# Eight places for weight steps in a gated batch, an early first chunk, and a re-ordered channel MLP

## The chip, the cores and the metric

The kernel runs on one core of one Trainium2 chip. The metric is the time of the device in microseconds (us), smaller is better; the outputs have to match the reference within float32-like accuracy, which the kernel reaches by splitting each float32 operand of a matmul into a high and a low part ("fp32r" in the rows) and multiplying three combinations.

## The reference

Three layers follow each other on 8 batches of 576 positions and 512 channels (8 heads of 64).

```
k_p, q_p = phi(k), phi(q)                       # linear attention, 128 features, exp(+-)
attn = (q_p @ (k_p.T @ v)) / (q_p . sum(k_p))
h = relu(x @ w_in); u, v = h[..., :512], h[..., 512:]
v_s = w_spatial @ layernorm(v) + b_spatial      # mixes positions
x = (u * v_s) @ w_out                           # gated MLP
u = x + (x.T @ U @ V).T                         # rank 32 mix of positions
out = u + relu(u @ w_ch1) @ w_ch2               # channel MLP, 512 -> 2048 -> 512
```

## The kernel before

**Stages.** The program is one straight line of instructions. The attention ends at about 388 us of the span. Then come eight gated batches, b0 to b7, of some 65 us each, and from 925 us the channel MLP.

**A gated batch.** On TensorE (PE): `pu` (x times w_in for u; ACT applies the relu, L907), then `pz` (w_spatial times the normalized v). DVE multiplies `pz` by u in place (L928), and ACT and POOL split the product into the parts of `gs` (L146, L149). Then `px` (gs times w_out) for four tiles of 128 positions and a fifth of 64, which shares a product with its low part (L790; "tail" below). ACT copies each px into x (L960), DVE splits x into xh and xl (L148, L149), and PE goes on with the rank 32 mix: `pr` (L974, L976), `pt` and `py` (L996 to L1000), the sum going to DRAM as `ud`. The values `v` of the next batch (`pv`, L839 to L856) lie between. A scheduler places these stages; within an engine the order is fixed once the kernel is built.

**Weight steps.** The channel MLP's weights have to be expanded from an integer form, split and written to DRAM beside the batches. `channel_jobs` makes lists of jobs per batch: *pieces* of w_ch1 and rows of w_ch2 (each a DMA in, L53; ACT L62 and L80; DVE L67, L71, L75, L87; a DMA out, L359), *pairs* (two such fetches, sums on POOL L457, a split into `w2s` in two parts that share one buffer, each stored as `w2d`, L415) and *lefts* (the same sums and splits for w_ch1, `w1s`, stored to `w1x`, L439). `work()` pops one step; `gate` calls it once per f in its first loop (4 calls) and, in its second loop, once per f but the last (3 calls), with one more step pending per pair of calls.

**Channel MLP.** It is a two-level scheme with 7 products each way. For each of 16 chunks n, `channel` issues the outer products `pc` from the left parts w (a DMA w<-w2d, L1286) and the right parts `hc` (hidden values split, L146, L149). Between them it pulls steps of the generator `inner`, which makes the hidden values of the coming chunk: for each of 4 tiles t, seven products into two PSUM tiles, X (`ph_x`, products 0, 1, 3, 6) and Y (`ph_y` with product 4, then `ph_z` with 2 and 5). X is read after each of its first three products by ACT (copies s1, u2, u3, L1148), DVE adds such a copy to Y (c, L1153), and ACT writes relu(c) or relu(X) into `h` (L1161). The chunk's input u (DMA u<-ud, 1152 KB) is summed on POOL (t, L1089) and split into `us` (ACT L146, DVE L149) by `right_parts`, a generator whose steps are taken at the places (t, i) of a table, `spread` (`begin` for the first chunk). `second_group` loads, sums and splits the next left parts (ca, cs, cd) for half the chunks; `channel` takes its steps at 7 of 14 places (`later`). `rest` adds the products in DRAM terms (r, L1320). In this stage every engine's instructions are pinned to the program's order.

Of the kernel before, what the change touches and what calls it, by code (L numbers as in the profile page):

```python
# [18 lines left out]
P = 128  # L19
# [81 lines left out]
class Mixer:  # L101
# [243 lines left out]
    def channel_jobs(self):  # L345
# [99 lines left out]
        todo = [jobs[4 * m : 4 * m + 4] + [pair(m)] for m in range(GROUP)]  # L445
        todo += [jobs[4 * GROUP :], [left(m) for m in range(GROUP)]]
# [438 lines left out]
    def gate(self, b, jobs):  # L885
# [27 lines left out]
        for f in range(self.KH):  # L913
# [20 lines left out]
            if f < self.KH - 1:  # L934
                self.work()
# [151 lines left out]

    def less(self, out, p, q):
        self.put(self.nc.gpsimd.tensor_tensor(out=out, in0=p, in1=q, op=ALU.subtract))  # L1089
        return out  # L1090
# [36 lines left out]
    def hidden(self, n, m):  # L1127
# [55 lines left out]
        keep(3, c22[0])  # L1183
        keep(2, X)
        yield
# [4 lines left out]
    def inner(self):  # L1190
# [5 lines left out]
        for k in range(total):  # L1196
# [5 lines left out]
            for k, i in (  # L1202
                (0, 1), (1, 0), (0, 2), (1, 1), (0, 3), (1, 2), (0, 4), (1, 3), (1, 4),
                (0, 5), (0, 6), (1, 5), (1, 6), (2, 0),
# [6 lines left out]
                (2, 2), (2, 4), (2, 5), (3, 2), (3, 3), (3, 4), (4, 0), (3, 5), (4, 1), (4, 3),  # L1211
            )
        }
        for k, i in order:
# [13 lines left out]
            if (t, i) == (2, 2) and u is not None:  # L1228
                right, u = self.right_parts(n + 1, u), None
            at, steps = (k, i), begin  # L1230
            if k > GROUP + 1 or k == GROUP + 1 and i < 5:
                at, steps = (t, i), spread
                if t == 0 and (GROUP, i) in spread:
                    at = (GROUP, i)
            for _ in range(steps.get(at, 0)):
                next(right, None)
# [54 lines left out]
    def channel(self, inner):  # L1291
# [5 lines left out]
        for _ in range(7 * GROUP + FIRST - 7 * EARLY):  # L1297
            next(inner, None)
# [3 lines left out]
        def fill(f, into, n):  # L1302
            while len(into) < n:
                d = next(f, None)
                if d is None:
                    break
                into.append(d)
# [31 lines left out]

        fill(weights, ws, 5)  # L1340
        rest(0, 0, 0)
        rest(0, 0, 1)
        for n in range(total):
            for x in OUTER:
# [30 lines left out]
                for t in range(GROUP):  # L1375
# [19 lines left out]
                    if n and at in range(0, 14, 2):  # L1395
                        next(later, None)
# [3 lines left out]
def favor_gmlp_mixer_kernel(ctx: ExitStack, tc: tile.TileContext, **aps):  # L1400
# [11 lines left out]
    todo = [late] + jobs + [[]]  # L1412
    for t in range(NST):
        mx.values(0, t)
    for b in range(B):
        last = b == B - 1
        mx.gate(b, todo[b])
        if last:
            right.close()
            mx.alloc_channel(ctx)  # L1420
            u = mx.load_chunk(0)
            for m in range(GROUP):
                mx.load_left(m)
            right_parts = mx.right_parts(0, u)
            inner = mx.inner()
        else:
            for kk in range(KD):
                mx.load_x(b + 1, kk)()()
# [118 lines left out]
```

## Time and profile before

| | us |
|---|---|
| median of 3 runs (lowest, highest) | 1654.58 (1654.47, 1655.69) |
| the profiled execution | 1655.13 |
| span of its trace, from the first to the last instruction | 1653.3 |
| busy in the span: PE, DVE, ACT, POOL | 1574.3, 1177.9, 879.0, 793.9 |
| mean granted clock of PE | 0.992 |

The table is read from the top: the profiled execution lies 0.55 us above the median, inside the spread of the runs, so its rows stand for them. PE is busy 95% of the span, and no other engine comes near that. A granted clock of 1 is 2.4 GHz, 0.5 is 1.2 GHz.

### The profile page before, as it was taken

The page shows a single profiled execution, that of the slowest core. Times are in us where ns is not written, and L with a number is a line of the kernel's source. Part 1 is how long each engine was busy: PE and PEld are TensorE (multiplying, and loading weights), DVE is VectorE, ACT ScalarE, POOL GpSimd, SP SyncE. Part 2 cuts the span into 40 slices and gives each one's busy share as a digit, 9 for nine tenths or more (in the row PEclk, how much of TensorE's full clock was granted, in tenths as well). Part 3 has the DMA queues.
Part 4 walks back from the last instruction along what each step waited for, and adds up shares of the span by engine and source line. Part 5 has one row for each costly group of instructions (what it writes and reads, how often), then busy time and mean ns, then how long its engine had stood idle before and what let it go on. Part 6 is the DMA issues. An engine that isn't in the chain of part 4 may idle for free.

```text
span 1653.3 us, 30606 instructions
## 1 busy us (share of the span) xinstructions
PE 1574.3 (95%) x11592; PEld 1467.8 (89%) x11592; DVE 1177.9 (71%) x1642; ACT 879.0 (53%) x1668; POOL 793.9 (48%) x610
## 2 busy tenths in 40 slices
PE   7999999998999999898999899999999999999998
PEld 7998889888888787796988899999999999999998
DVE  6888757865576776757455678878877777767765
ACT  5888768773444444434434555555554455445443
POOL 3677766774342442442533346545543444433342
PEclk9999999999999999999999999999999999999999
DMA  4676666642252442523526668998899777777776
GB/s 136 194 205 203 201 186 179 197 141 70 70 162 88 144 147 88 173 89 121 193 84 249 226 222 267 317 325 293 298 330 389 258 223 225 244 251 234 250 240 231
DMA packets 172182, 336.72 MB, mean 204 GB/s; under 512 B 25794, under 2 KB 96610, under 8 KB 168964
## 3 DMA queue, kind: packets, MB, share of 16 engines
q1 hardware_dynamic: 171892, 334.72, 63.0%
q8 instruction: 91, 1.49, 0.4%
q14 instruction: 55, 0.45, 0.1%
q10 hardware_dynamic: 144, 0.07, 0.0%
HBM read 251.58 MB, written 73.55 MB: 197 GB/s over the span
## 4 chain that ended last, share of the span: by engine, by line
PE 53%; DVE 17%; DMA 14%; ACT 8%; issue 4%; POOL 2%; SPq 1%; DVEq 0%; ACTq 0%; POOLq 0%
PE pc L778 12%; PE ph_x L778 7%; PE pn L615 5%; PE pv L778 4%; PE pu L778 4%; PE pkv L587 4%; PE ph_z L778 4%; DVE hc L149 3%; DVE us L149 3%; DMA w<-w2d 2%; DMA w2d<-cd 2%; PE ph_y L778 2%; PE pk L514 2%; PE pt L546 2%; DMA raw_c<-in_w_ch 1%
## 5 line engine op out<-in xcount | busy, mean ns | idle before, releaser
L778 PE MATMUL pc<-hc,w 128*128 128x288 f32 x2688 | 422.4, 296 | 6.7 <-ACT hc L146 2.8
L778 PEld LDWEIGHTS pc<-hc,w 128*128 128x128 f32 x2688 | 379.2, 188 | 8.8 <-ACT hc L146 4.5
L778 PE MATMUL ph_x<-us,cw 128*128 128x288 f32 x1536 | 247.1, 296 | 9.8 <-ACT u L1148 7.0
L568 POOL TENSOR_TENSOR qp<-e,qp 128x576 fp32r<-128x576 f32 x128 | 183.9, 1458 | 121.1 <-ACT e L565 84.6
L778 PEld LDWEIGHTS ph_x<-us,cw 128*128 128x128 f32 x1536 | 217.6, 188 | 14.4 <-ACT u L1148 10.9
L615 PE MATMUL pn<-qp,kv 128*65 128x288 f32 x768 | 208.1, 331 | 10.2 <-DVE nd L624 6.7
L1089 POOL TENSOR_TENSOR t<-h,h 128x576 f32<-128x576 f32 x64 | 94.2, 1473 | 233.0 <-DVE hc L149 203.4
L149 DVE TENSOR_TENSOR hc<-t,hc 128x576 fp32r<-128x576 f32 x128 | 129.8, 1016 | 63.2 <-ACT hc L146 63.1
L1161 ACT ACTIVATE h<-c 128x288 f32<-128x288 f32 x192 | 85.7, 446 | 148.1 <-DVE c L1153 148.0
L587 PE MATMUL pkv<-v,kp 128*128 128x65 f32 x1024 | 153.8, 253 | 0.0
L587 PEld LDWEIGHTS pkv<-v,kp 128*128 128x128 f32 x1024 | 152.6, 192 | 0.0
L778 PE MATMUL ph_z<-us,cw 128*128 128x288 f32 x768 | 126.6, 299 | 8.6 <-DVE c L1153 8.4
L1148 ACT COPY u<-ph_x 128x288 f32<-128x288 f32 x128 | 51.0, 398 | 150.0 <-PE ph_x L778 149.9
L778 PEld LDWEIGHTS ph_z<-us,cw 128*128 128x128 f32 x768 | 107.8, 188 | 13.4 <-DVE c L1153 10.7
L1089 POOL TENSOR_TENSOR t<-h,t 128x576 f32<-128x576 f32 x64 | 113.1, 1768 | 8.3 <-DVE hc L149 5.8
L149 DVE TENSOR_TENSOR hc<-h,hc 128x576 fp32r<-128x576 f32 x96 | 115.6, 1208 | 1.9 <-ACT hc L146 1.9
L1089 POOL TENSOR_TENSOR t<-u 128x576 f32<-128x576 f32 x32 | 49.8, 1558 | 136.0 <-DVE us L149 116.6
L615 PEld LDWEIGHTS pn<-qp,kv 128*65 128x65 f32 x768 | 99.2, 140 | 16.2 <-DVE nd L624 8.1
L778 PE MATMUL pz<-wt,vn 128*128 128x288 f32 x768 | 112.6, 295 | 0.9 <-DVE u L928 0.9
L149 DVE TENSOR_TENSOR us<-t,us 128x576 fp32r<-128x576 f32 x64 | 85.0, 1331 | 36.1 <-ACT us L146 35.3
L778 PE MATMUL pu<-xs,wi 128*128 128x288 f32 x768 | 105.5, 299 | 4.3 <-DVE v L842 4.3
L778 PEld LDWEIGHTS pu<-xs,wi 128*128 128x128 f32 x768 | 104.9, 191 | 5.3 <-DVE v L842 4.5
(169 smaller groups left out, 3193.2 us busy)
## 6 DMA issues: line engine op xcount, KB each, us to landing
w<-w2d SPq DMA_DIRECT2D x224, 512.0 KB, 4.8
u<-ud SPq DMA_DIRECT2D x16, 1152.0 KB, 5.6
raw_c<-in_w_ch SPq DMA_DIRECT2D x32, 512.0 KB, 4.1
cw<-w1x SPq DMA_DIRECT2D x8, 1792.0 KB, 10.8
v<-in_v SPq DMA_DIRECT2D x32, 325.0 KB, 4.1
k<-in_kT SPq DMA_DIRECT2D x32, 320.0 KB, 3.5
q<-in_qT SPq DMA_DIRECT2D x32, 320.0 KB, 3.7
x<-nd SPq DMA_DIRECT2D x64, 144.0 KB, 3.2
```

The costliest lines, as they stand in the source:

```text
L149: return self.put((nc.gpsimd if elo == "pool" else nc.vector).tensor_tensor(out=lo, in0=src, in1=hi, op=ALU.subtract))
L514: self.pin(nc.tensor.matmul(pa[:, j * NF + t, :], x[d, t * P : (t + 1) * P], ws[d, :], start=True, stop=True,))
L546: self.pin(nc.tensor.transpose(pt[:, at, :], s[:, u, :], self.ident))
L568: self.pin(nc.gpsimd.tensor_tensor(out=lo[:, c], in0=e[:, c], in1=hi[:, c], op=ALU.subtract))
L587: self.pin(nc.tensor.matmul(pkv[:, i, j, :], kp[:, j * NF + t, :], vb[:, u * D1 : (u + 1) * D1], start=False, stop=(j == 1 and t == NF - 1),))
L615: self.pin(nc.tensor.matmul(pn, kv[k][:, i, g // 2, :], qp[q][:, i, g * HS : (g + 1) * HS], start=(m == 0), stop=(m == len(terms) - 1),))
L778: self.put(self.nc.tensor.matmul(out, x, y, start=(start and i == 0), stop=(stop and i == len(terms) - 1), skip_group_check=chained,))
L1089: self.put(self.nc.gpsimd.tensor_tensor(out=out, in0=p, in1=q, op=ALU.subtract))
L1148: self.put(nc.scalar.copy(out, src))
L1161: self.put(nc.scalar.activation(self.h[n, t // 2, x][:, t % 2], src, AF.Relu))
```

## The change

Eight edits: (A) `channel_jobs` deals its jobs to the batches in another way: b0 gets the remainder of an earlier job list plus two pieces, b1 to b4 three pieces and a pair each, b5 seven pieces, b6 three pieces and two lefts, b7 (nothing before) two lefts. (B) The second loop of `gate` calls `work()` after the first two f only. (C) `first_chunk` loads the first chunk's u into the buffer of the last batch's xs, and not into a buffer of its own. (D) In `hidden` the relus of X and of c22 are issued one product later, X's first. (E) Two neighbours in `inner`'s early order are exchanged. (F) `right_parts` of the coming chunk is made at (1, 6) and not at (2, 2), and its steps are taken at other places. (G) The first outer form is filled after the 23rd step of the channel's early pulls, not after all of them. (H) `second_group`'s steps come at other places of 14.

```diff
@@ -442,8 +442,9 @@
                 return (lambda: part(w, z, 1)) if k == 0 else None
             return load
 
-        todo = [jobs[4 * m : 4 * m + 4] + [pair(m)] for m in range(GROUP)]
-        todo += [jobs[4 * GROUP :], [left(m) for m in range(GROUP)]]
+        lefts = [left(m) for m in range(GROUP)]
+        todo = [jobs[:2]] + [jobs[3 * m + 2 : 3 * m + 5] + [pair(m)] for m in range(GROUP)]
+        todo += [jobs[14:21], jobs[21:] + lefts[:2], lefts[2:]]
         return todo
 
     def left_sums(self, blocks, z):
@@ -931,7 +932,7 @@
                 lo = self.split(gs[:, 0, f, cs], gs[:, 1, f, cs], u, elo=elo)
                 self.last[2 if elo == "pool" else 1] = lo.ins
 
-            if f < self.KH - 1:
+            if f < self.KH - 2:
                 self.work()
         self.gs, self.gt = gs, self.last_tokens(self.mp, gs, f"gt_{b}")
 
@@ -1083,6 +1084,12 @@
     def load_chunk(self, n):
         u = self.hu.tile([P, self.KD, self.S], F32, tag="u32", name=f"u32_{n}", bufs=1)
         self.nc.sync.dma_start(u, self.ud[n % self.B])
+        return u
+
+    def first_chunk(self):
+
+        u = self.wp.tile([P, 2, self.KD, self.S], F32, tag="xs", name="u32_0", bufs=1)[:, 0]
+        self.nc.sync.dma_start(u, self.ud[0])
         return u
 
     def less(self, out, p, q):
@@ -1180,9 +1187,7 @@
         c22 = []
         yield lambda: c22.append(plus(Y, u3))
         product(X, 6, False, True)
-        keep(3, c22[0])
-        keep(2, X)
-        yield
+        yield lambda: (keep(2, X), keep(3, c22[0]))
         product(Y, 5, False, True)
         c12 = plus(Y, u2)
         yield lambda: keep(1, c12)
@@ -1200,15 +1205,15 @@
         order[a:z] = [
             (EARLY + k, i)
             for k, i in (
-                (0, 1), (1, 0), (0, 2), (1, 1), (0, 3), (1, 2), (0, 4), (1, 3), (1, 4),
-                (0, 5), (0, 6), (1, 5), (1, 6), (2, 0),
+                (0, 1), (1, 0), (0, 2), (1, 1), (0, 3), (1, 2), (0, 4), (1, 3), (0, 5),
+                (1, 4), (0, 6), (1, 5), (1, 6), (2, 0),
             )
         ]
         pairs, late, right, u = {}, None, iter(()), None
         begin = {(2, 3): 1, (2, 5): 1, (2, 6): 1, (3, 6): 2, (4, 0): 2, (4, 2): 1, (4, 3): 1, (4, 4): 1}
         spread = {
             x: 1 for x in (
-                (2, 2), (2, 4), (2, 5), (3, 2), (3, 3), (3, 4), (4, 0), (3, 5), (4, 1), (4, 3),
+                (1, 6), (2, 3), (2, 6), (3, 2), (3, 3), (4, 0), (3, 5), (3, 6), (4, 1), (4, 3),
             )
         }
         for k, i in order:
@@ -1225,13 +1230,13 @@
             late = after
             if (t, i) == (1, 1) and n + 1 < groups * B:
                 u = self.load_chunk(n + 1)
-            if (t, i) == (2, 2) and u is not None:
-                right, u = self.right_parts(n + 1, u), None
             at, steps = (k, i), begin
-            if k > GROUP + 1 or k == GROUP + 1 and i < 5:
+            if k > GROUP:
                 at, steps = (t, i), spread
                 if t == 0 and (GROUP, i) in spread:
                     at = (GROUP, i)
+            if at == ((2, 3) if steps is begin else (1, 6)) and u is not None:
+                right, u = self.right_parts(n + 1, u), None
             for _ in range(steps.get(at, 0)):
                 next(right, None)
             if i == 6 and (n + 1) % B == 0 and g + 1 < groups:
@@ -1294,8 +1299,6 @@
         nc, HS, B, S = self.nc, self.HS, self.B, self.S
         total = self.NM // GROUP * B
         self.pinning = True
-        for _ in range(7 * GROUP + FIRST - 7 * EARLY):
-            next(inner, None)
         forms, weights, later = self.operands(), self.outer_weights(), self.second_group()
         ready, ws, rs = [], [], {}
 
@@ -1337,6 +1340,10 @@
         def banks(name, tag):
             return self.ps["c"].tile([P, 2, 512], F32, tag=tag, name=name, bufs=1)[:, :, :HS]
 
+        for i in range(7 * EARLY, 7 * GROUP + FIRST):
+            next(inner, None)
+            if i == 22:
+                fill(forms, ready, 1)
         fill(weights, ws, 5)
         rest(0, 0, 0)
         rest(0, 0, 1)
@@ -1392,7 +1399,7 @@
                         pulls += (LEAD - FIRST) // 4
                     for _ in range(pulls):
                         next(inner, None)
-                    if n and at in range(0, 14, 2):
+                    if n and at in (1, 3, 5, 6, 9, 11, 12):
                         next(later, None)
 
 
@@ -1409,7 +1416,7 @@
 
     mx.alloc_moe(left, right)
     jobs = mx.channel_jobs()
-    todo = [late] + jobs + [[]]
+    todo = [late + jobs[0]] + jobs[1:]
     for t in range(NST):
         mx.values(0, t)
     for b in range(B):
@@ -1418,7 +1425,7 @@
         if last:
             right.close()
             mx.alloc_channel(ctx)
-            u = mx.load_chunk(0)
+            u = mx.first_chunk()
             for m in range(GROUP):
                 mx.load_left(m)
             right_parts = mx.right_parts(0, u)
```

**ACT, batch b1.** Before: x products of b1 are copied at L960 (px, four tiles); g is the split of gs, gt a copy of its last part, w2 and z2 the two sources of the pair's store.

```order
L146 CAST g_1_5553<-u1_2_5471 128x288
L62 ACTIVATE low_c2_0_1_5684<-raw2_c2_0_1_5638 128x512
L146 CAST g_1_5553<-u1_3_5512 128x288
L80 ACTIVATE low_c2_0_1_5684<-raw2_c2_0_1_5638 128x512
L146 CAST g_1_5553<-u1_3_5512 128x288
L800 COPY gt_1_5733<-g_1_5553 128x4x64
L146 CAST w2s_0_0_5933<-w2_0_5599 128x512
L800 COPY gt_1_5733<-g_1_5553 128x4x64
L146 CAST w2s_0_0_5933<-w2_0_5599 128x256
L146 CAST w2s_0_1_6003<-z2_0_5692 128x1024
L960 COPY x_1_0_5783<-px1_0_5753 128x512
L960 COPY x_1_1_5792<-px1_1_5763 128x512
```

ACT at the same place after the change (lines of after from L442 on are higher by one or more):

```order
L146 CAST g_1_5577<-u1_2_5495 128x288
L62 ACTIVATE low_c2_0_1_5660<-raw2_c2_0_1_5614 128x512
L146 CAST g_1_5577<-u1_2_5495 128x288
L80 ACTIVATE low_c2_0_1_5660<-raw2_c2_0_1_5614 128x512
L146 CAST g_1_5577<-u1_3_5536 128x288
L146 CAST w2s_0_0_5945<-w2_0_5574 128x512
L146 CAST w2s_0_0_5945<-w2_0_5574 128x256
L146 CAST g_1_5577<-u1_3_5536 128x288
L801 COPY gt_1_5745<-g_1_5577 128x4x64 x2
L146 CAST w2s_0_1_6015<-z2_0_5668 128x1024
L961 COPY x_1_0_5795<-px1_0_5765 128x512
```

The first source's two casts now stand ahead of the last g and gt; the second one (w2s_0_1), which fills the same buffer as the first, still stands ahead of the four x copies.

**ACT, batch b7.** Before, from the last g on; us0 to us6 are the right parts of chunk 0, s1 and u2 the copies of its first hidden product.

```order
L146 CAST g_7_9574<-u7_3_9545 128x288 x2
L800 COPY gt_7_9719<-g_7_9574 128x4x64 x2
L960 COPY x_7_0_9774<-px7_0_9744 128x512
L960 COPY x_7_1_9787<-px7_1_9754 128x512
L960 COPY x_7_2_9799<-px7_2_9764 128x512
L146 CAST us0_0_9796<-u32_0_9734 128x576
L146 CAST us4_0_9808<-u32_0_9734 128x576
L960 COPY x_7_3_9811<-px7_3_9813 128x512
L146 CAST us2_0_9830<-t1_0_9783 128x576
L792 COPY lowx7_9844<-px7_4_9835 64x512
L146 CAST us1_0_9867<-t2_0_9785 128x576
L146 CAST us3_0_9890<-t3_0_9849 128x576
```

ACT at the same place after the change:

```order
L146 CAST g_7_9569<-u7_3_9530 128x288 x2
L801 COPY gt_7_9719<-g_7_9569 128x4x64 x2
L146 CAST us0_0_9796<-u32_0_9734 128x576
L146 CAST us4_0_9808<-u32_0_9734 128x576
L146 CAST us2_0_9830<-t1_0_9783 128x576
L146 CAST us1_0_9867<-t2_0_9785 128x576
L146 CAST us3_0_9890<-t3_0_9849 128x576
L146 CAST us6_0_9900<-t2_0_9785 128x576
L146 CAST us5_0_9911<-u32_0_9734 128x576
L961 COPY x_7_0_9774<-px7_0_9744 128x512
L961 COPY x_7_1_9787<-px7_1_9754 128x512
L961 COPY x_7_2_9799<-px7_2_9764 128x512
```

All seven us now stand ahead of the first x copy of the last batch.

**DVE, the end of chunk n = 8's hidden products** (c8_7 belong to it; us are the right parts of chunk 9, hc7 the outer right parts). Before:

```order
L149 TENSOR_TENSOR us2_9_14829<-t1_9_14676,us2_9_14829 128x576
L149 TENSOR_TENSOR us1_9_14849<-t2_9_14678,us1_9_14849 128x576
L149 TENSOR_TENSOR hc7_5_0_14852<-h3_7_0_13891,hc7_5_0_14852 128x576
L1153 TENSOR_TENSOR c8_7_14872<-ph8_7_z_14832,u38_7_14847 128x288
L149 TENSOR_TENSOR us3_9_14889<-t3_9_14839,us3_9_14889 128x576
L149 TENSOR_TENSOR hc7_5_1_14892<-h3_7_2_14193,hc7_5_1_14892 128x576
L1153 TENSOR_TENSOR c8_7_14909<-ph8_7_z_14832,u28_7_14826 128x288
```

DVE at the same place after the change:

```order
L149 TENSOR_TENSOR us2_9_14829<-t1_9_14637,us2_9_14829 128x576
L149 TENSOR_TENSOR hc7_5_0_14849<-h3_7_0_13907,hc7_5_0_14849 128x576
L1160 TENSOR_TENSOR c8_7_14869<-ph8_7_z_14832,u38_7_14847 128x288
L149 TENSOR_TENSOR us1_9_14871<-t2_9_14639,us1_9_14871 128x576
L149 TENSOR_TENSOR hc7_5_1_14887<-h3_7_2_14209,hc7_5_1_14887 128x576
L1160 TENSOR_TENSOR c8_7_14904<-ph8_7_z_14832,u28_7_14826 128x288
L149 TENSOR_TENSOR us3_9_14908<-t3_9_14839,us3_9_14908 128x576
```

Each of the two c that read ph8_7_z has one us fewer ahead of it: us1_9 and us3_9 now follow.

## Rows read from the trace of the kernel before

**Rows 1.** Waits of PE, b1 to b3 (456:651): engine line <- releaser: us, times, longest.

```profile
PE px L790 <- ACT x L960: 6.3, 3, 2.2
PE px L778 <- DVE u L928: 3.6, 3, 1.2
```

**Rows 2.** Waits of PE, b4 (651:719).

```profile
PE px L790 <- ACT x L960: 2.0, 1, 2.0
PE pr L976 <- DVE xl L149: 1.4, 3, 0.8
```

**Rows 3.** Waits of PE, b5 (719:787).

```profile
PE pr L976 <- DVE xl L149: 2.3, 2, 1.8
PE pv L790 <- ACT uo L1003: 1.0, 1, 1.0
```

**Rows 4.** Waits of PE, b7 (849:925).

```profile
PE ph_x L778 <- ACT s L1148: 2.6, 1, 2.6
```

**Rows 5.** Waits of PE, first chunk (925:980).

```profile
PE pc L778 <- DVE hc L149: 2.8, 1, 2.8
PE pc L778 <- ACT hc L146: 1.2, 1, 1.2
```

**Rows 6.** Waits of PE, chunks 1 to 7 (980:1311).

```profile
PE ph_z L778 <- DVE c L1153: 8.2, 9, 1.7
PE ph_x L778 <- ACT u L1148: 3.7, 8, 0.5
PE pc L778 <- DMA w<-w2d: 0.8, 1, 0.8
```

**Rows 7.** Waits of PE, chunks 8 to 14 (1311:1640).

```profile
PE ph_x L778 <- ACT u L1148: 2.9, 6, 0.5
```

**Rows 8.** Stretches: us; busy us of PE, PEld, DVE, ACT, POOL; PE clock; DMA share; GB/s.

```profile
980.00:1311.00 331.00, 318.30 (x2354) 312.73 (x2353) 262.50 (x313) 173.87 (x376) 170.47 (x116) 1.00 0.90 309
1311.00:1640.00 329.00, 324.96 (x2422) 321.48 (x2421) 232.90 (x288) 160.63 (x342) 134.29 (x84) 1.00 0.77 248
```

**Rows 9.** The same for stretches in b4, b5 and ahead of the channel MLP.

```profile
698.00:703.00 5.00, 4.40 (x12) 3.23 (x12) 3.60 (x7) 0.00 (x0) 0.07 (x1) 0.66 0.00 0
763.00:769.00 6.00, 5.33 (x16) 3.95 (x17) 5.20 (x10) 1.58 (x3) 0.00 (x0) 0.72 0.36 101
926.00:932.00 6.00, 3.44 (x16) 3.44 (x17) 6.00 (x5) 0.89 (x3) 5.43 (x4) 0.72 0.69 236
```

**Rows 10.** Waits of PE, b0 (388:456).

```profile
PE pz L778 <- DVE u L928: 0.9, 1, 0.9
```

**Rows 11.** Timeline of ACT in b1: start us, duration, operation, idle before and its releaser.

```profile
497.08 1.04 ACT L146 CAST w2s<-z 128x1024 fp32r<-128x1024 f32 x1 [4.20 <-DMA w2d<-w2s]
```

**Rows 12.** Timeline of POOL in b4.

```profile
695.76 1.18 POOL L457 TENSOR_TENSOR z<-z,w 128x256 f32<-128x256 f32 x1
```

**Rows 13.** Waits of PE, b6 (787:849).

```profile
PE pr L976 <- DVE xl L149: 1.1, 3, 0.5
```

**Rows 14.** Timeline of ACT in chunk 8.

```profile
1346.75 0.39 ACT L1161 ACTIVATE h<-ph_x 128x288 f32<-128x288 f32 x1
...
1351.59 0.45 ACT L1161 ACTIVATE h<-c 128x288 f32<-128x288 f32 x1 [3.31 <-DVE c L1153]
...
1353.08 0.39 ACT L1148 COPY u<-ph_x 128x288 f32<-128x288 f32 x1
```

**Rows 15.** Timeline of DVE in chunk 8.

```profile
1349.21 1.98 DVE L149 TENSOR_TENSOR hc<-h,hc 128x576 fp32r<-128x576 f32 x1
1351.11 0.45 DVE L1153 TENSOR_TENSOR c<-ph_z,u 128x288 f32<-128x288 f32 x1
```

**Rows 16.** DVE's L149, 1311:1640: duration ns min/median/max, first and last start.

```profile
L149 DVE TENSOR_TENSOR hc<-t,hc x64: 741/759/1735, 1318.5 to 1639.4; 128x576 fp32r<-128x576 f32 x64
...
L149 DVE TENSOR_TENSOR us<-t,us x24: 758/1538/1926, 1342.4 to 1580.8; 128x576 fp32r<-128x576 f32 x24
```

**Rows 17.** Timeline of PE in chunk 8.

```profile
1348.13 0.95 PE L778 MATMUL ph_y<-us,cw 128*128 128x288 f32 x6
```

## The prediction, made before the changed kernel ran

> **What bounds the kernel now.** I read the busy times first: PE works 1574 of the 1653 us of the span (the table above), 95%, so the change can only win what PE waits for and what its clock loses. I then read PE's waits stage by stage, since each stage waits for another engine; the reader is to look at the releaser and the total. In b1 to b3 PE waits for ACT's x copies and DVE's products with u, 9.9 us together [rows 1]; in b4 and b5 for x, xl and uo [rows 2, 3]; in b7 once, 2.6 us, for the copy s1 of the first hidden product [rows 4]; at the first outer products for their right parts hc, 2.8 and 1.2 us [rows 5]. In the channel MLP it waits 14 times about half a microsecond for a u copy (8 + 6 times, 3.7 + 2.9 us) [rows 6, 7], and in chunks 1 to 7 another 8.2 us for c [rows 6]. In these chunks PE is idle 331 - 318.3 = 12.7 us, in 8 to 14 only 329 - 325.0 = 4.0 [rows 8]. Last I looked for half clock: three stretches near the edits show a mean clock of 0.66, 0.72 and 0.72 over 5, 6 and 6 us [rows 9], that is 5 x 0.34 = 1.7, 6 x 0.28 = 1.7 and again 1.7 us of PE time lost, each behind a wait of the same stage. All of this together is some 45 us; the other PE time is matmuls that the change leaves as they are.
>
> **The change part by part.** The matmuls are the same and in nearly the same order, so the sum is one of waits. ACT, DVE and POOL get the same operations at other places; no operation goes.
>
> *b0* (A, B): two pieces more, whose DVE steps fall between the pz products. The product with u is late by 0.9 us now [rows 10]; one more step ahead of it could double that. Cost 0.9, bounds 0 and 3.
>
> *b1 to b3* (A, B): In b1 the second source of the pair, w2s_0_1, waits 4.20 us for the store of the first out of the same buffer; its cast is in front of the four x copies, and PE's tail waits for those [rows 11]. The third place of the second loop goes, so a piece less stands between the last pz products, and the first source's casts move ahead of the last g. The store then starts one to two microseconds earlier; but the second source is still ahead of the x copies, and the store's own latency stays. I take the 1.2 us u wait and a little of the 2.1 us x wait in each: 1.5 x 3 = 4.5. Bounds 0 (the chain of store and cast moves with the rest) and 9.9 [rows 1].
>
> *b4*: the same pair, and xl waits 1.4 us [rows 2] behind sums on POOL [rows 12] that begin when the second source is split. If x comes earlier, these sums and the splits still follow the same release, so I take the 1.5 of the batches before and about half of 1.4 + 1.7 (the clock [rows 9]): 3.0. Bounds 0 and 2.0 + 1.4 + 1.7 = 5.1.
>
> *b5*: eight rows now, one of them between the splits of xh and xl; seven pieces after, none there. The waits 2.3 and 1.0 [rows 3] and the clock's 1.7 [rows 9] would go, 5.0; the pieces still pass one raw buffer one after the other, so I take 4.0. Bounds 0 and 5.0.
>
> *b6*: three pieces and two lefts instead of four lefts. The sums of a left on POOL now stand between the g of u6_2, which px needs: four such sums at 1.2 us each or a little less [rows 12] could hold it up. The 1.1 us of waits for xl [rows 13] may go at the same time. Net cost 1.0, bounds -1.1 and 4.
>
> *b7* (A, C): the first chunk's u no longer waits for the first left part on SP's queue, so the seven us casts on ACT, and their sums on POOL, run ahead of x_7_0. The 2.6 us for s1 [rows 4] goes. In exchange the x copies stand behind the seven casts, and two lefts sit in the batch; what they make late is px's tail and pr. No row shows by how much. I take the size of an x wait in b1 to b3, 6.3 / 3 = 2.1 [rows 1], a little lowered because the chunk's u lands before the last g: 2.6 - 1.6 = 1.0, bounds -3 and 2.6.
>
> *The channel's start* (G): the first outer form is split while the early pulls go on, so the 1.2 and 2.8 us [rows 5] and the 1.7 us of half clock behind them [rows 9] lose their cause. The right parts of chunk 1, split there as well, are likely to be late next by 2 to 3 us. Of 5.7 I take 3.0, bounds 0 and 5.7.
>
> *The u copies* (D, F). In chunk 8 the copy stands on ACT behind a relu of c which idles 3.31 us for it [rows 14]; that c is on DVE behind a right part hc of 1.98 us [rows 15] and, ahead of that, us3. After the change us1 and us3 each follow the c that they preceded. One subtraction of a us lasts 1.54 us in the median [rows 16], so c, the relu and the copy behind it come some 1.5 us earlier, and the wait is 0.5. All 14 should go: 3.7 + 2.9 = 6.6; I take 6.5. Bounds 0 and 6.6.
>
> *The c in chunks 1 to 7* (F, H). 8.2 us in 9 waits [rows 6]. Two kinds: behind `second_group`'s split cd, whose step moves from one place to the next, and behind the us splits that now begin at (1, 6). The first kind should go; at the second, the same splits still lie ahead of c in the order. I take half, 4.1; bounds -4 (a new place for each step may hit another c) and 8.2.
>
> One rule speaks against the last two terms. What the rows show is that the same subtraction takes 741 ns at best and 1926 at most, and us, which is split beside POOL's t, is at 1538 in the median while hc from t is at 759 [rows 16]. The Trainium skill, page "SBUF — State Buffer", section "Who interferes with whom", with the reading notes above it, says that VectorE operations with two SBUF inputs and GpSimd share a pair of ports under an exclusive lock, the loser standing still for the whole instruction. By it moving steps in time saves nothing unless POOL's work moves off them too; the sum would lose the 4.1 and perhaps half of the 6.5. The rows agree that a slow form exists beside POOL; they don't show that the new places meet more of it.
>
> *D, E alone* cost no work: relu X is issued behind product 5 of Y, not behind its own last product. What hides that is one matmul group (rival 3).
>
> Sum: -0.9 + 4.5 + 3.0 + 4.0 - 1.0 + 1.0 + 3.0 + 6.5 + 4.1 = 24.2. From the profiled execution's 1655.1 that gives 1630.9; it stands 0.55 above the median of the runs, so I say 1630.5.
>
> **The rivals.**
>
> 1. *The channel MLP doesn't move.* DVE and POOL do the same work in the same chunks and c is late at another place. For: DVE is busy 79% of the time in chunks 1 to 7 (262.5 of 331 us) [rows 8], and the slow forms of us. Against: in chunks 8 to 14 DVE is less loaded and the only wait is the copy. It takes away 6.5 + 4.1: 1655.1 - 13.6 = 1641. The rule quoted above would lead here. Chance 0.16.
>
> 2. *The batches don't gain.* The chain fetch, expand, store, split keeps its length, and the x copies stay behind it. For: the 4.20 us wait is a transfer, not an engine's work [rows 11]. Against: b5 loses its steps among the splits altogether. It takes away 4.5 + 3.0 + 4.0: 1655.1 - 12.7 = 1642. Chance 0.14.
>
> 3. *The other side: X's buffer comes free too late.* With the relu of X behind product 5, the next X or Y that takes this PSUM buffer waits. In chunk 8 the relu of X starts at 1346.75, and the next pair's ph_y at 1348.13 [rows 14, 17], so about 1.38 - 0.39 = 1.0 us is left now; one product more of six matmuls takes 0.95 [rows 17]. If the copies ahead push the relu past what is left in all 64 tiles (16 chunks of 4), each 0.5 us over costs 32 us: 1655.1 - 24.2 + 32 = 1663. It decides from 0.4 us over in each tile (24.2 / 64). Against: the code gives these tiles a ring of four buffers. Chance 0.03.
>
> 4. *It does nothing*, each wait being replaced by one of its size: the DMA share of these chunks is already 0.90 [rows 8], and w<-w2d ended one wait of 0.8 us [rows 6]; if those transfers bound chunks 1 to 7, and the batches' new waits eat the rest: 1655 ± 3. Chance 0.06.
>
> **How the numbers follow.** My forecast has 0.61: its own range, from the terms' bounds taken half together, is 1620 to 1640. The rivals 1 and 2 lie at 1641 and 1642 and rival 3 and 4 beyond; below, all upper bounds together would be -24.2 + (9.9 - 4.5) + (5.1 - 3.0) + 1.0 + 2.1 + 1.6 + 2.7 + 0.1 + 4.1 = about 19 us more, 1612. I give 1614 to 1648, which leaves out rivals 3 and 4 and the ends. Within 0.2% of 1654.6 (3.3 us), which is about what a measurement here can tell from no change, lie rival 4 and a little of 1 and 2: same 0.07; slower 0.05; faster 0.88.
>
> **What would show it.** In the changed trace: no wait of ph_x for a u copy in chunks 8 to 14, and PE's idle time there below 1.5 us; the c waits of chunks 1 to 7 at about 4; no 2.6 us wait for s1 in b7, but a pr or px tail of 1 to 2 us; x copies in b1 to b3 behind a wait for w2d of 2 to 3 us rather than 4.20; the clock full in b5; the pc waits at the start under 3 us together. Wrong would be: ph_x waiting for a relu (rival 3), c waits above 8 (rival 1), or the px tails at 2 us as before (rival 2).

## The result, and the profile after

The changed kernel takes 1634.95 us in the median of 4 runs (1628.22 to 1638.32), against 1655.13 (4 runs, 1654.47 to 1662.64) for the kernel before. The medians differ by 20.2 us, a ratio of 0.988; the ratio of the means, which is given with a 95% interval here and below, is 0.9863 (0.982 to 0.9905). The forecast took 24.2 us off the profiled execution; the measured time lies in its range, 4.5 us above the 1630.5 that it names.

The profiled execution is the fastest of the four, 1628.22 us, 26.9 below the profiled execution of before. Cut at the first pu of each batch and the first pc of chunks 0, 1, 7 and 15 in both traces, it goes:

| stage, us | before | after | difference | forecast |
|---|---|---|---|---|
| attention | 388.43 | 383.82 | -4.6 | 0 |
| b0 | 67.57 | 68.40 | +0.8 | +0.9 |
| b1 to b3 | 194.66 | 189.38 | -5.3 | -4.5 |
| b4 | 68.43 | 64.57 | -3.9 | -3.0 |
| b5 | 67.61 | 66.91 | -0.7 | -4.0 |
| b6 | 62.37 | 66.50 | +4.1 | +1.0 |
| b7 | 76.34 | 72.80 | -3.5 | -1.0 |
| chunk 0 (the channel's start) | 54.01 | 51.57 | -2.4 | -3.0 |
| chunks 1 to 6 | 285.45 | 280.05 | -5.4 | together |
| chunks 7 to 14 | 359.38 | 353.24 | -6.1 | -10.6 |
| the rest | 29.09 | 29.20 | +0.1 | 0 |

The attention is the same code in the same order; its 4.6 us are no gain of the change (last section). Without it the trace gains 22.3 us, near the 20.2 of the medians.

The page of the changed kernel, part 1: PE has 11.2 us less of busy time than before with as many matmuls, and 15.7 us less of idle time. The clock explains at most 5.4 us of the busy time: the trace of before has 25.5 us at half clock and this one 14.8, and at most half of such a stretch is lost. Another part is waits that the rows count as work: in chunks 1 to 14, where neither trace has half clock, 65 matmuls last over 0.35 us before and 23 after (the median is 0.29), and PE's busy time falls by 5.5 us.

```profile
PE 1563.1 (96%) x11592; PEld 1462.6 (90%) x11592; DVE 1170.4 (72%) x1642; ACT 883.0 (54%) x1668; POOL 807.8 (50%) x610
```

The waits of PE in b1 to b6 of the changed kernel (452 to 840 us):

```profile
PE px L791 <- ACT x L961: 6.3, 4, 3.0
PE px L779 <- DVE u L929: 6.2, 7, 1.6
PE pr L977 <- DVE xl L149: 3.6, 6, 1.5
PE pr L975 <- DVE xh L148: 0.7, 2, 0.4
```

The px tails have 6.3 us as b1 to b3 had alone [rows 1], but now most of it is in two batches, 3.0 in b5 and 1.9 in b6; b1 to b3 have 1.4. What changed in b1 to b3 is this row of ACT in b1, to be read beside [rows 11]:

```profile
491.91 1.05 ACT L146 CAST w2s<-z 128x1024 fp32r<-128x1024 f32 x1 [3.67 <-DMA w2d<-w2s]
```

The second source still stands ahead of the x copies, but it waits 3.67 us for the store and not 4.20, and starts 39.7 us after the batch's first pu and not 41.1. Of the channel's start, where pc waited [rows 5], this is left (912 to 964 us):

```profile
PE ph_x L779 <- DVE us L149: 3.3, 2, 2.4
```

The pc waits have gone, and the hidden products now wait for chunk 1's us. In chunks 1 to 7 (964 to 1289 us), to be read beside [rows 6]:

```profile
PE ph_z L779 <- DVE c L1160: 8.5, 6, 2.9
PE pc L779 <- DVE hc L149: 0.9, 1, 0.9
PE pc L779 <- ACT hc L146: 0.3, 1, 0.3
```

The u copies have left the list, and c has not: 8.2 us in 9 waits became 8.5 in 6. The stretches of chunks 1 to 7 and 8 to 14, with [rows 8] before, have as columns us, busy us of PE, PEld, DVE, ACT and POOL, clock, DMA share and GB/s:

```profile
964.00:1289.00 325.00, 315.29 (x2356) 312.04 (x2356) 259.57 (x313) 176.72 (x376) 179.37 (x117) 1.00 0.91 315
1289.00:1597.00 308.00, 308.00 (x2315) 306.35 (x2314) 218.78 (x273) 156.82 (x333) 136.19 (x82) 1.00 0.78 248
```

From 1289 to 1597 us PE is never idle; the stretch of before had 4.0 us of idle time.

### The profile page after: what moved, and what is told of

Its sections match the earlier page's. It is cut to its first block, busy times and chain, and to the rows that moved or that the text cites. A ratio compares the mean times of both kernels' runs of the same rounds, so it can differ in the third digit from the quotient of the medians.

```text
span 1626.4 us, 30538 instructions
## 1 busy us (share of the span) xinstructions
PE 1563.1 (96%) x11592; PEld 1462.6 (90%) x11592; DVE 1170.4 (72%) x1642; ACT 883.0 (54%) x1668; POOL 807.8 (50%) x610
## 4 chain that ended last, share of the span: by engine, by line
PE 69%; DVE 12%; DMA 8%; ACT 5%; issue 3%; POOL 2%; SPq 1%; DVEq 0%; ACTq 0%; POOLq 0%
PE pc L779 19%; PE ph_x L779 11%; PE ph_z L779 6%; PE pv L779 5%; PE pn L616 5%; PE pkv L588 4%; PE pu L779 4%; PE ph_y L779 3%; PE pk L515 2%; PE pt L547 2%; DMA raw_c<-in_w_ch 2%; DMA w1d<-w_c 1%; PE pq L515 1%; PE pt L997 1%; DVE bits_c L67 1%
## 5 line engine op out<-in xcount | busy, mean ns | idle before, releaser
L1096 POOL TENSOR_TENSOR t<-h,h 128x576 f32<-128x576 f32 x64 | 113.4, 1773 | 183.0 <-DVE hc L149 164.7
L149 DVE TENSOR_TENSOR hc<-t,hc 128x576 fp32r<-128x576 f32 x128 | 132.2, 1035 | 50.2 <-ACT hc L146 49.9
L149 DVE TENSOR_TENSOR hc<-h,hc 128x576 fp32r<-128x576 f32 x96 | 125.0, 1305 | 9.6 <-ACT hc L146 9.5
L779 PEld LDWEIGHTS pz<-wt,vn 128*128 128x128 f32 x768 | 105.2, 188 | 3.1 <-DVE u L929 3.1
```

Of the source, the lines that this page charges most:

```text
L149: return self.put((nc.gpsimd if elo == "pool" else nc.vector).tensor_tensor(out=lo, in0=src, in1=hi, op=ALU.subtract))
L779: self.put(self.nc.tensor.matmul(out, x, y, start=(start and i == 0), stop=(stop and i == len(terms) - 1), skip_group_check=chained,))
```

## The experiments

Every run below is one kernel with some of the eight edits, or the changed kernel with another edit on top. Medians go with the ratio of the means to the kernel before on the same chip. Since one kernel's runs on one chip differ by 4 to 13 us (last section), parts are judged by stages of the trace, in the table's cuts. Where a stretch at half clock falls into a stage it is named; half of its length is taken as lost, which is the most that it can cost. A and B were only run together, and E was not run by itself.

**The weight steps alone (A, B).** The kernel before with these edits of the diff: the new `todo`, `KH - 2` in `gate`, and `todo = [late + jobs[0]] + jobs[1:]`.

> The kernel before with the new dealing of the weight steps and the eight places alone (edits A and B). My theory, that a batch's time is set by where its own steps stand: the stages of the trace move as they did in the changed kernel, b0 +0.8, b1 to b3 together -5.3, b4 -3.9, b5 -0.7, b6 +4.1 us, in sum -4.9, the channel MLP not at all: about 1650. Rival: the batches gain only with the other edits, because the scheduler lays them out anew: their sum is within 2 us of before, 1655.

1647.1 us, ratio 0.9961 (0.9941 to 0.9982). b1 to b3 187.98 us, b4 64.60, b5 66.75, as in the changed kernel; b6 64.29; chunks 1 to 6 285.10 and 7 to 14 359.28, as before. b0 to b6 together gain 10.6 us where I said 4.9. Of the excess of 5.7, b6 has 2.2: it loses 1.9 us and not 4.1, without the 3.4 us at half clock that the changed kernel has there (1.7 lost). b0 has 2.0, at the same 3.4 us of half clock: PE waits there 3.1 us for v and 1.4 for u, in the changed kernel 4.4 and 2.2. Why these differ between two kernels with the same edits in b0 I did not trace. The gain in b1 to b4 is A and B's own.

**D alone.**

```diff
-        keep(3, c22[0])
-        keep(2, X)
-        yield
+        yield lambda: (keep(2, X), keep(3, c22[0]))
```

> The kernel before with the relus of X and c22 one product later, and nothing else (edit D). My theory: the u copies wait on ACT behind a relu of c that DVE makes late behind us and hc, and D alone doesn't move those; the 14 waits of ph_x, 6.6 us together, stay, and the time is within 2 us of before. Rival: the relu that held the copy is one of the two moved, and D alone takes the 6.6 us away: 1648. Second rival, the predicted slower side: X's buffer is free too late, ph_x or ph_y waits for a relu in 64 tiles, over 1663.

1641.41 us, ratio 0.993 (0.9904 to 0.9956). My theory fell: the waits for the u copies go with D alone. Chunks 1 to 6 take 277.95 us and 7 to 14 352.38, 14.5 us less than before and 3.0 less than in the changed kernel. ACT in this run, at the place of [rows 14]:

```profile
1332.34 0.40 ACT L1148 COPY s<-ph_x 128x288 f32<-128x288 f32 x1
1332.81 0.68 ACT L146 CAST us<-t 128x576 fp32r<-128x576 f32 x1
1333.39 0.67 ACT L146 CAST hc<-h 128x576 fp32r<-128x576 f32 x1
1333.97 0.40 ACT L1161 ACTIVATE h<-ph_x 128x288 f32<-128x288 f32 x1
1334.47 0.45 ACT L1161 ACTIVATE h<-c 128x288 f32<-128x288 f32 x1
1338.28 0.44 ACT L1161 ACTIVATE h<-c 128x288 f32<-128x288 f32 x1 [3.36 <-DVE c L1153]
...
1339.77 0.39 ACT L1148 COPY u<-ph_x 128x288 f32<-128x288 f32 x1
```

The cast of us3 (1332.81) now precedes both relus. In the trace of before the relu of c22 stood there first, idle for 1.73 us until c22 came, with that cast queued behind it, and DVE waited for the cast in turn:

```profile
1346.40 0.44 ACT L1161 ACTIVATE h<-c 128x288 f32<-128x288 f32 x1 [1.73 <-DVE c L1153]
1347.04 0.67 ACT L146 CAST us<-t 128x576 fp32r<-128x576 f32 x1
1347.74 1.55 DVE L149 TENSOR_TENSOR us<-t,us 128x576 fp32r<-128x576 f32 x1 [1.38 <-ACT us L146]
```

With D alone DVE does this split without a wait:

```profile
1334.36 1.61 DVE L149 TENSOR_TENSOR us<-t,us 128x576 fp32r<-128x576 f32 x1
```

So the next c starts 3.8 us after c22 and not 5.2. ACT still idles 3.36 us before that c's relu, but relu and u copy lie early enough for PE. No wait for a relu of X appeared: the predicted slower side is excluded at these places.

**F alone.** `right_parts` is made at (1, 6), and its steps go to the new `spread`.

> The kernel before with right_parts' places alone (edit F). My theory: c no longer stands behind a us on DVE, so the copies come 1.5 us earlier and the 14 waits of ph_x go without D: chunks 8 to 14 lose 0.8 us each, as in the changed kernel, 6.6 to 9 us in all, 1646 to 1648. Rival: D and F are both needed, half of the waits or more stay: 1651 to 1655. The c waits of chunks 1 to 6 stay at 8 to 9 us by both.

1648.56 us, ratio 0.9959 (0.9938 to 0.998). Of the waits for u copies 0.2 us are left in chunks 1 to 6, and none behind; c has 6.5 us in 9 waits, less than the 8 to 9 that both theories left it. Chunks 1 to 6 take 280.47 us, 7 to 14 355.03. So F suffices for the copies too; D and F take the same wait by two ways, and their gains don't add.

**Without C.** The changed kernel with `u = mx.load_chunk(0)`.

> The changed kernel with the first chunk's u in a buffer of its own again, behind the first left part on SP's queue (without C). My theory: the wait of 2.6 us for s1 in b7 comes back, and b7 is 3 to 4 us longer than in the changed kernel's trace (72.8), everything else the same. Rival: two lefts in b7 hold its x copies anyway, so b7 stays within 1 us of 72.8.

1638.2 us, ratio 0.9909 (0.9882 to 0.9936). The wait of ph_x for s1 is back at 2.5 us, and b7 takes 75.02 us, 2.2 more than with C: the theory's wait, at two thirds of the size I gave. Chunks 1 to 6 (282.73) hold 6.8 us at half clock, 3.4 lost.

**Without F.** The changed kernel with the old `spread` and (2, 2).

> The changed kernel with right_parts' old places (without F). Theory from the runs with D alone and F alone: D already frees the u copies, and F on top of it only puts more DVE work ahead of the c in chunks 1 to 6. Then chunks 1 to 6 take about 278 us (280.05 in the changed kernel's trace, 277.95 with D alone), chunks 7 on 352.4 to 353.2, and the time is 2 to 3 us below the changed kernel's. Rival, my prediction's step: F is what takes the us from ahead of the c; without it part of the 0.65 us waits comes back, 3 to 6 us longer than the changed kernel.

1636.17 us, ratio 0.9881 (0.9852 to 0.991). Chunks 1 to 6 take 284.93 us, 4.9 more than with F (3.4 of it at half clock, so 1.7 lost), though the u copies cost nothing (0.3 us in one wait). Neither is right: the stage loses what the rival said, but not by the wait that it named, since PE waits 9.5 us for c instead; and the loss that I had read from the run with D alone isn't F's. In this stage the kernel differs from D alone by H only, and is 7.0 us slower, 1.7 of them the clock.

**Without H.**

```diff
-                    if n and at in (1, 3, 5, 6, 9, 11, 12):
+                    if n and at in range(0, 14, 2):
```

> The changed kernel with second_group's old places (without H). Theory: the waits for c that were left in chunks 1 to 6 lie behind the splits cd and hc that the same chunk needs anyway, so H only moves them: chunks 1 to 6 within 1 us of 280.05. Rival, my prediction's step: H takes the waits behind cd, which then come back, 2 to 4 us longer.

1623.35 us, ratio 0.9817 (0.9774 to 0.986). Both theories fell: without H this stage is shorter. Chunks 1 to 6 take 274.96 us, 5.1 less. The median of the whole is 11.6 us below the changed kernel's, but the two intervals overlap, so the stage is what shows it. It is also 3.0 us below D alone, which in these chunks lacks F, so F gains there once H is out. The c waits fall from 8.5 us to this (969 to 1244 us of the run):

```profile
PE ph_z L779 <- DVE c L1160: 2.3, 3, 1.2
PE pc L779 <- DMA w<-w2d: 1.9, 2, 1.8
```

The place where c is late shows why. DVE in the changed kernel, up to the c for which PE waited 2.9 us (chunk 6):

```profile
1216.01 1.99 DVE L149 TENSOR_TENSOR hc<-t,hc 128x576 fp32r<-128x576 f32 x1
1217.92 0.74 DVE L1323 TENSOR_TENSOR r<-pc,r 128x576 f32<-128x576 f32 x1
1218.58 1.32 DVE L149 TENSOR_TENSOR us<-u,us 128x576 fp32r<-128x576 f32 x1
1219.82 1.91 DVE L149 TENSOR_TENSOR cd<-cs,cd 128x512 fp32r<-128x512 f32 x1
1221.66 1.95 DVE L149 TENSOR_TENSOR hc<-t,hc 128x576 fp32r<-128x576 f32 x1
1223.53 0.44 DVE L1160 TENSOR_TENSOR c<-ph_z,u 128x288 f32<-128x288 f32 x1
```

And without H:

```profile
1216.43 1.70 DVE L149 TENSOR_TENSOR cd<-cs,cd 128x512 fp32r<-128x512 f32 x1 [0.36 <-ACT cd L146]
1218.05 0.74 DVE L1323 TENSOR_TENSOR r<-pc,r 128x576 f32<-128x576 f32 x1
1218.72 1.32 DVE L149 TENSOR_TENSOR us<-u,us 128x576 fp32r<-128x576 f32 x1
1219.96 0.74 DVE L149 TENSOR_TENSOR hc<-t,hc 128x576 fp32r<-128x576 f32 x1
1220.63 0.45 DVE L1160 TENSOR_TENSOR c<-ph_z,u 128x288 f32<-128x288 f32 x1
```

H puts a split cd between us and the hc ahead of c; it lasts 1.91 us, and hc behind it 1.95 instead of 0.74. The moved step costs itself and makes its neighbour meet a difference t on POOL (1221.15 to 1223.00 in the changed kernel; without H POOL has none under that hc, its last one ending at 1219.43). The long splits are no fewer without H: 62 of 126 exceed 0.95 us in both kernels. So 6.2 us of the c waits are a matter of order alone.

**H alone.** The kernel before with the new places of `later`.

> The kernel before with second_group's new places alone (edit H). Theory from the run without H: H costs by itself, chunks 1 to 6 take 290 us or more (285.45 before), since its splits of cd fall beside more of POOL's differences and hc. Rival: H costs only in the changed kernel, where D moved the relus; alone it is within 1.5 us of before, or gains the 4.1 us of my prediction.

One run, 1666.47 us. Chunks 1 to 6 take 291.12 us against 285.45, with two half-clock stretches of 3.4 us. The c waits of this stage rise (984 to 1276 us) from 8.2 to:

```profile
PE ph_z L778 <- DVE c L1153: 10.7, 8, 2.4
```

So H costs by itself, 2.5 us in c waits and, with up to 3.4 for the clock, 5.7 in the stage; the theory's 290 us are reached only with the clock.

The clock goes with these waits. In chunks 1 to 6 of the six traces with H and POOL's differences, PE ran at 1.2 GHz for 0 us (the changed kernel's own), once for 3.4 and four times for 6.8; of the seven without H, six have none and one 3.4. Every one of these stretches begins during a wait of PE of 1.7 to 3.1 us or within 1.2 us of its end. In the runs without C, with x first and with b6's order alone it is the wait for c in chunk 6 shown above, of 2.9 to 3.1 us, and PE is at half clock for 6.8 us at its end. The changed kernel's profiled execution has that wait and no such stretch, so its trace shows less of H's cost than others. Not every wait of that length is followed by one.

**POOL without reads.** Every difference t on POOL becomes a fill of the same tile; the values of t are left out.

```diff
-        self.put(self.nc.gpsimd.tensor_tensor(out=out, in0=p, in1=q, op=ALU.subtract))
+        self.put(self.nc.gpsimd.memset(out, 0.25))
```

> The changed kernel with every difference t on POOL replaced by a fill of the same tile, so POOL writes in these steps and reads nothing (the output is not the reference's; the rest of the work is the same). Theory A, that DVE's splits stand still beside a POOL operation that reads: the long forms of us, hc and cd (1.3 to 2.0 us) fall to 0.75, and with them the c waits of chunks 1 to 6 (8.5 us) to under 2. Theory B, that the c waits come from the order on DVE alone: the c waits stay at 6 to 9 us although POOL reads nothing.

One run, 1619.3 us. Theory A: no c wait is left in chunks 1 to 6 (nor any but 2.6 us for a transfer w<-w2d), and chunks 1 to 5 take 44.46 us each. DVE's splits in chunks 1 to 6 of the changed kernel (duration min/median/max in ns):

```profile
L149 DVE TENSOR_TENSOR hc<-t,hc x48: 741/755/1992, 972.1 to 1227.9; 128x576 fp32r<-128x576 f32 x48
L149 DVE TENSOR_TENSOR hc<-h,hc x37: 739/1572/1991, 963.4 to 1243.5; 128x576 fp32r<-128x576 f32 x37
L149 DVE TENSOR_TENSOR us<-t,us x24: 741/857/1254, 997.0 to 1238.8; 128x576 fp32r<-128x576 f32 x24
L149 DVE TENSOR_TENSOR us<-u,us x18: 743/1320/1982, 984.3 to 1241.6; 128x576 fp32r<-128x576 f32 x18
```

And in this run:

```profile
L149 DVE TENSOR_TENSOR hc<-t,hc x48: 743/751/1296, 971.5 to 1214.5; 128x576 fp32r<-128x576 f32 x48
L149 DVE TENSOR_TENSOR hc<-h,hc x36: 748/752/1298, 961.0 to 1229.9; 128x576 fp32r<-128x576 f32 x36
L149 DVE TENSOR_TENSOR us<-t,us x24: 748/754/760, 995.3 to 1229.2; 128x576 fp32r<-128x576 f32 x24
L149 DVE TENSOR_TENSOR us<-u,us x18: 746/750/791, 960.4 to 1212.1; 128x576 fp32r<-128x576 f32 x18
```

The median of hc from h falls from 1572 to 752 ns, and no us exceeds 0.79 us. The 11 splits over 0.95 us that stay in 960 to 1231 us (8 of hc, 3 of cd) all overlap a left sum on POOL (L458), which still reads. In the changed kernel all 62 splits of 128x576 over 0.95 us in chunks 1 to 6 overlap an operation of POOL, and of the 64 shorter ones 48 overlap none. A fill takes 0.58 us where a difference took 1.4 to 2.0, so a split meets it more rarely; but 23 of the splits of 128x576 in this run do overlap a fill, and all 23 take 0.75 to 0.76 us, while of the splits that overlap a difference in the changed kernel 55 are long and 7 short. So it is POOL's reading, not its being busy, that goes with the long forms. What the run cannot separate is how much of the c waits goes because t is there earlier: a fill waits for no input. Theory B is not refuted as a second cause: the run without H took most of the c waits away by order alone, with the long forms as they were.

**The first outer form alone (G).** The kernel before with `fill(forms, ready, 1)` behind the 23rd early step.

> The kernel before with the first outer form ahead of the last early pulls (edit G alone). Theory: G alone takes the pc waits of 2.8 and 1.2 us and shortens the first chunk from 54.0 to about 51.5, with new waits of ph_x for us of 1 and 2.6 us as in the changed kernel. Rival: the first chunk gains because C brings u earlier, and G alone leaves it at 53 to 54.

One run, 1654.02 us. The pc waits go and ph_x waits 3.6 us for us in their place, as in the changed kernel; chunk 0 takes 54.25 us with one half-clock stretch of 3.4 us in it, as before (54.01 with one). G trades 4.0 us of waits for 3.6 us of others; the changed kernel's 51.57 is the stage without such a stretch, and that makes 1.7 of its 2.4 us. C, the rival, is not what does it: without C chunk 0 takes 51.58 us.

**x first.** The changed kernel with the steps behind a batch's output products held behind the x copies, and b6's jobs in another order. Two of the eight places are calls of `work()` within the rank 32 mix. In the program they stand behind the x copies, but a step there is only held behind the copy gt and the last split of gs, so the scheduler could put it in front of an x copy.

```diff
-            nc.scalar.copy(x, px)
-            self.split(xh, xl, x, ehi="dve", elo="dve")
+            self.last[0] = nc.scalar.copy(x, px).ins
+            self.last[1] = self.split(xh, xl, x, ehi="dve", elo="dve").ins
...
-        todo += [jobs[14:21], jobs[21:] + lefts[:2], lefts[2:]]
+        todo += [jobs[14:21], lefts[:1] + jobs[21:] + lefts[1:2], lefts[2:]]
```

> The changed kernel with two edits in the batches: a weight step that is due after a batch's output products may be issued only behind the last x copy and the last xl split, and b6 takes its lefts around the three pieces. Theory: the px tails of b1, b3, b5 and b6 (0.8, 0.8, 3.2, 2.1 us) and the xl waits of b4 and b6 stand behind weight steps that wait for a transfer on ACT; with x first b5 loses 2 to 5 us and b6 3 to 4, and b1 to b4 together 2 to 4: 7 to 11 us in the stages of the trace, about 1626. Rival: the steps issued later hold the next batch's v or the output copies uo instead, and b1 to b6 gain less than 3 us together.

1621.31 us, ratio 0.9792 (0.9774 to 0.981). b1 to b4 together 250.33 us (253.95 in the changed kernel), b5 64.59, b6 61.16: 11.3 us less in these six, of which 3.4 are the clock (10.2 us at half clock in the changed kernel's b5 and b6, 3.4 here). b5's 2.3 us are all clock (6.8 us at half clock against 1.0): PE's wait for x falls there from 3.0 to 1.1 us, but a wait of 2.4 us for the output copy uo comes instead, as the rival had it. The rest is 3.6 us in b1 to b4 and 4.8 in b6, and what it removes is on ACT. In the changed kernel's b5, a piece waits for its transfer in front of an x copy:

```profile
748.37 1.55 ACT L961 COPY x<-px 128x512 f32<-128x512 f32 x3
752.70 0.70 ACT L62 ACTIVATE low_c<-raw_c 128x512 int32<-128x512 uint32 x1 [2.78 <-DMA raw_c<-in_w_ch]
753.31 0.56 ACT L961 COPY x<-px 128x512 f32<-128x512 f32 x1
```

and in b6 the second part of a left does so for the store of its first:

```profile
807.50 0.96 ACT L801 CAST gt<-g 128x256 fp32r<-128x256 f32 x2
812.06 1.04 ACT L146 CAST w1s<-z 128x1024 fp32r<-128x1024 f32 x1 [3.61 <-DMA w1x<-w1s]
813.01 1.56 ACT L961 COPY x<-px 128x512 f32<-128x512 f32 x3
```

**b6's order alone.** Only the second piece of that diff.

> The changed kernel with b6's lefts around its pieces and nothing else. Theory: most of b6's loss is the second part of a left that stands ahead of the x copies; with another left's part there in its place the wait stays, b6 is 64 to 66.5, and what gained with x first was the order of the x copies. Rival: the order of the jobs is the cause, and b6 falls to 61 to 62 us without holding any step behind x.

One run, 1633.8 us. b6 takes 63.03 us, 3.5 less (1.7 of it the clock), and has no px tail any more; the waits for xl and xh stay (1.5 and 0.4 us). It lies between the two theories: the wait at the px tail, which mine kept, is gone by the order alone, but 61 to 62 us are not reached. With the clock taken off, of b6's 4.8 us the order gives 1.8 and x first 3.0. The other batches' gain needs x first; x first without this order was not run.

**Both together.** x first, b6's order, and without H.

> The changed kernel with x first in the batches and b6's lefts around its pieces, and second_group's old places (the edits of the two runs that beat it, together; without H). Theory: they act in different stages and add up: b1 to b6 about 376 us as with x first, chunks 1 to 6 about 275 as without H; 16 us below the changed kernel's stages, near 1616 in the median. Rival: the times of the channel depend on when the batches end (transfers of w2d), and the sum gains under 10 us.

1618.38 us, ratio 0.9778 (0.9754 to 0.9802): the lowest median of the kernels that keep the computation, though its interval overlaps that of x first. b1 to b6 take 379.2 us (387.4 in the changed kernel), with 6.9 us at half clock in b5 and b6, and chunks 1 to 6 273.31. These stages gain 14.9 us of the 16 expected, so the two edits add up and the rival falls. Its waits of PE in b1 to b6:

```profile
PE px L779 <- DVE u L929: 6.0, 6, 1.6
PE py L1001 <- DVE t L985: 3.5, 4, 0.9
PE pv L791 <- ACT uo L1004: 2.7, 1, 2.7
PE px L791 <- ACT x L961: 0.9, 1, 0.9
```

No pr waits are left and one px tail; 3.5 us of the gain is given back to py, which waits for t, and 2.7 to the wait for uo. As to t: in b1 of the run with x first, DVE's split of the second source (2.27 us) now stands ahead of it.

## Why the prediction was right, and where its steps were not

*b0.* The 0.8 us against 0.9 is luck: the u wait grew from 0.9 to 2.2 us, and 3.4 us less at half clock hid the difference. The trace of before has 6.8 us at half clock in b0, which the prediction did not count.

*b1 to b3, b4.* The direction and the sizes held, 5.3 and 3.9 us against 4.5 and 3.0, and the run of A and B alone shows them as these edits' own. But the u waits of 1.2 us, of which I took all, did not go: 3.6 us in three waits became 4.4 in five. What went is the x wait, 6.3 to 1.4 us, of which I took a little: the store's wait in front of the x copies became 0.5 to 1.3 us shorter and began earlier. So the right sum came from the wrong half.

*b5.* "Seven pieces after, none there" failed, and so did the full clock in b5 that was to show it. Two of the eight places stand behind the output products, pieces are still due there, and one's transfer was waited for in front of the last x copy: 2.78 us on ACT, 3.0 on PE, and PE's clock was at half for 6.8 us around it. Gain 0.7, not 4.0.

*b6.* Expected was a wait for POOL's sums at g; the sums took 0.74 us each and PE lost nothing there. What cost time is the chain of cast, store and second cast in front of the x copies, the one I had described for b1 to b3: 1.9 us of waiting for x, and 1.7 for the clock, of the 4.1; with the lefts in another order 3.5 of them go.

*b7 and the start.* The wait for s1 went; the price I set against it, 1.6 us, was 0.6. At the start the us of chunk 1 are late next, as foreseen; the waits only changed places (G alone), and the 2.4 us of chunk 0 are mostly the clock.

*The u copies.* All 14 waits went, 6.6 us by the rows of waits; chunks 8 to 14 are each some 0.8 us shorter from first pc to first pc. The step named as the cause, us behind c through F, is enough (F alone); but D alone does it too, by another queue: on ACT the relu of c22, idle for its c, no longer holds the cast of us3 behind it. I had booked D at nothing.

*The c in chunks 1 to 7.* The step that failed is H's: it was to take the waits behind cd, and it put a cd ahead of another c. 4.1 us were forecast and -0.3 measured; the sign set for rival 1, c waits above 8, is met with 8.5. H alone makes the waits longer, and without H 2.3 us of them are left in chunks 1 to 6, less than the 4 that I expected. The Trainium skill's rule in "SBUF — State Buffer", section "Who interferes with whom", is half of the account. This case's rows agree with it on the slow form: when POOL reads nothing, DVE's long splits next to its differences are gone, and the c waits with them. That moving steps saves nothing, which the prediction drew from it, is not borne out: without H the long splits are as many and the c waits fall by 6.2 us.

Rival 2 is excluded for b1 to b4 by the run of A and B, but its sign, px tails of 2 us, stands in b5 and b6; rival 3 is excluded by D alone, rival 4 by the result. The time came out near the forecast because b7 and the chunks' copies gained 2.5 and about 5 us more than I took while b5, b6 and c gave 3.3, 3.1 and 4.4 less. That these cancel is luck: no step of the prediction ties them together.

## What to carry to other kernels

Before moving a step to "other places", list what stands right behind it on its engine and who waits for that: one split in front of the wrong c cost 1.9 us of its own and 1.2 us more of its neighbour, and one fetch in front of an x copy 3 us. Steps that wait for a transfer belong behind the copies that PE needs, not at the next free place; then look at what they hold there, as uo in b5. And test each edit of a bundle alone: here one of eight cost 5 us in its stage, and two took the same 6.6 us of waits.

## What the hardware showed that I had not expected

The attention, the same instructions in every kernel here, took from 383.8 to 395.9 us. Its stretch from the start to the first pu, of the changed kernel, of the kernel before and of F alone, in this order (clock in the third column from the end):

```profile
0.00:383.80 383.80, 363.89 (x3416) 330.56 (x3417) 283.99 (x343) 287.02 (x410) 258.07 (x200) 1.00 0.64 182
```

```profile
0.00:388.40 388.40, 366.34 (x3416) 332.76 (x3417) 283.92 (x343) 288.42 (x415) 257.69 (x200) 0.99 0.63 180
```

```profile
0.00:395.90 395.90, 373.37 (x3416) 339.76 (x3417) 283.49 (x345) 287.72 (x414) 258.01 (x200) 0.98 0.62 177
```

The granted clock is at 1.2 GHz for none, twice 3.4 and 13.7 us of the three, by the trace's own list of clock changes. At most half of that is lost: 0, 3.4 and 6.8 of the 0, 4.6 and 12.1 us by which the three differ; the other 1.2 and 5.3 us I did not trace. So such stretches fall differently from trace to trace in a stage whose code is the same. Runs of one kernel on one chip spread over 4 to 13 us, and their mean clock goes with it: of the changed kernel's four, the fastest (1628.22 us) has 0.995 and the slowest (1638.32) 0.987. Effects of 2 us could only be read from stages. The forecast's sum counted three stretches as the change's to win, and part of that was luck: b5's did not go but grew to 6.8 us, and the one at the start is there again with G alone and with x first.
